# Two x tiles by DMA transposes, one tile's statistics on ScalarE, and finer-grained products at the head of a token-mixing MLP kernel

## The chip, the cores and the metric

The kernel runs on one core of a Trainium2 chip. The metric is the device time of one execution in microseconds, as the median of several runs. The engines are named as in the profile: PE (TensorE, matmuls), PEld (its weight loads), DVE (VectorE), ACT (ScalarE), POOL (GpSimd) and SP (SyncE, which here only issues DMAs).

## The reference

```python
B, S, D, F = 1, 2048, 512, 1792          # everything in bf16

def reference(x, w1, w2, w3, w4):
    h = _gelu(_layernorm(x, axis=-1) @ w1)             # D -> D
    c = D // 4                                         # four groups of 128 channels,
    g0 = h[..., 0*c:1*c] shifted by +1 along S         # zero padded at the ends
    g1 = h[..., 1*c:2*c] shifted by -1
    g2 = h[..., 2*c:3*c] shifted by +2
    g3 = h[..., 3*c:   ] shifted by -2
    x1 = x + jnp.concatenate([g0, g1, g2, g3], axis=-1) @ w2
    return x1 + _gelu(_layernorm(x1, axis=-1) @ w3) @ w4
```

(The four shifts are written here in words; the original pads and slices.)

## The kernel before

The 2048 rows are 16 tiles of 128 rows. Row p*16+t belongs to partition p of tile t, so that a shift along S by one or two rows is, but for the edges, a step to the neighbouring tile. The work of a tile goes through these stages:

- **Statistics** on DVE: `stats` (L325, "st") gives partial means and variances, `aggr` (L328, "ag") merges them. **Power** on POOL: `rstd_pool` ("rs") adds epsilon (L349) and raises to -0.5 (L358). **Normalization** on DVE: `norm` (L378) writes the bf16 tile `xn`; for the second layer norm some tiles are normalized by ACT (L373) instead, for which POOL also makes a negative mean (L354) and its product with the power (L363).
- **Transposes** of `xn` into `xT`, by one of two paths. `peT` (L400, "tp") transposes four 128x128 blocks on PE into a PSUM bank, and `evacT` on ACT (L412, "evA") copies the bank to SBUF. `dmaT` (L388, "dT") issues one DMA transpose from SP's queue. Before, tiles 0 to 7 go over PE and tiles 8 to 15 by DMA.
- **First products** `mm1` (L451): for a pair p of tiles (2p and 2p+1), 16 matmuls of 256 columns each into two PSUM banks, in four groups by output chunk. Pair 0 has a form of its own, `mm1_by_input` (L467), which goes through the input chunks in the outer loop, so that it can begin with the first half of w1. `gelu1` on ACT (L495, L501, L512) writes the result to `hT`.
- **Second products** `mm2` (L526): for a tile, four matmuls of 512 columns that read the four channel groups of `hT` at the neighbouring tiles' places (`window`), summed in one PSUM bank. `add1` on DVE (L538) adds x and writes `x1`.
- **Second layer norm**: the same statistics on `x1`, in the order of tiles 2, 3, ..., 15, 0, 1 (numbered 16 to 31 in the program), all transposed by DMA into `x1T`.
- **Wide products**: `mm3` (L553) with w3 for 512 rows at a time (s = 0 to 3), `gelu2` (L566) on ACT, and `mm4` (L579) with w4; `add2` (L593) adds `x1` and SP writes the tile out. Before it can begin, `mm3` needs all of w3 and the first four tiles of `x1T`.

There is no scheduler: each engine does its operations in the order in which the Python program records them. For the head (up to the first layer norm's last tile) this order is written by hand as one string, `HEAD`, a list of steps such as `st 4` or `m1 2 0 1` (pair 2, banks from 0, output chunk 1), which all engines share; each engine takes from it what is its own, in order. What follows it is a sequence of Python calls. `emit` finds what each operation depends on, from the tiles that it reads and writes, and puts a semaphore wait ahead of it (L134) where the dependence isn't known to be met. A PSUM bank or a buffer that is used again waits for the readers of its last use.

All loads stand in SP's queue, in this order: x tiles 0 to 3 one by one, tiles 4 and 5, w1 in two halves, tiles 6 and 7, tiles 8 to 11, tiles 12 to 15, w2; then the DMA transposes of `xT`, w3, the DMA transposes of `x1T`, and w4 in four parts between the last of these. `keep_warm` (L611) fills the start of PE with matmuls on constants: 12 at the beginning and 3 more once the variance of tile 3 is there.

Of the kernel before, what the change touches and what calls it, by code (L numbers as in the profile page):

```python
# [5 lines left out]
P = 128  # L6
ACT_F = mybir.ActivationFunctionType
ALU = mybir.AluOpType
# [152 lines left out]
st 0; ag 0; rs 0 1; st 1; ag 1; rs 1 1; st 2; st 3; ag 2; ag 3; warm 3 3 1; rs 2; norm 1; norm 0;  # L161
tp 1 5; tp 0 4; st 4; evA 1; norm 2; norm 3; evA 0; tp 2 6; tp 3 7; st 5; ag 4; ag 5; m1i 0 0 0;
evA 3; rs 4; m1i 0 0 1; evA 2; m1i 0 0 2; st 6; m1i 0 0 3; norm 4; m1 1 4 3; norm 5; g1 0;
tp 4 6; st 7; m1 1 4 0; ag 6; ag 7; tp 5 7; rs 6; evA 4; m1 1 4 1; st 9; evA 5; m1 1 4 2; st 8;
norm 7; m1 2 0 1; ag 8; ag 9; g1 1; m1 2 0 3; rs 8; norm 6; tp 7 7; st 11; m1 2 0 2; evA 7;
tp 6 6; norm 8; m1 2 0 0; ag 11; evA 6; m2 2 4 0; m2 2 4 1; st 10; m1 3 2 2; norm 9; ag 10; g1 2;
m1 3 2 0; rs 10; st 13; m1 3 2 1; m1 3 2 3; st 12; m2 2 4 2; dT 8; m2 2 4 3; norm 11; ag 13;
norm 10; g1 3; m2 3 5 0 1 2 3; st 14; ag 12; dT 9; rs 12; st 15; m2 4 6 0 1 2 3; ag 14; ag 15;
m1 4 0 3; rs 14; dT 11; m1 4 0 1; norm 13; m1 4 0 0; add 3; norm 14; dT 10; m2 5 7 0 1 2 3;
add 2; m1 4 0 2; norm 12; norm 15; dT 13; g1 4; dT 12; dT 14; dT 15  # L170
# [3 lines left out]
def bass_standalone__mixer_s_mlp__prompt_kernel(  # L174
# [26 lines left out]
    with ExitStack() as es:  # L201
# [11 lines left out]
        ident = sb("ident", [P, P], BF16)  # L213
        xn = sb("xn", [P, NXN, D], BF16)
# [61 lines left out]
        def consts():  # L276
# [8 lines left out]
            pr.op("pool", "eps", lambda e: e.memset(eps_c[:], LN_EPS), w=[g_eps])  # L285
            pr.op("pool", "nh", lambda e: e.memset(neghalf[:], -0.5), w=[g_nh])
# [44 lines left out]
        g_sd = {}  # L331
# [34 lines left out]

        def norm(eng, q):
# [3 lines left out]
            if eng == "act":  # L371
# [3 lines left out]
                      r=[g, g_nmr[q], g_rstd[q]], w=[g_xn[q]])  # L375
            else:
# [82 lines left out]
        def mm1_by_input(p, b, dcs):  # L459

            if p not in g_y:
                g_y[p] = ([bank[b + i].new() for i in range(DC)], b)
            for dc in dcs:
                def f(e, dc=dc):
                    for fc in range(DC):
                        dst = ps[:, 512 * (b + fc) : 512 * (b + fc) + 256]
                        ins = e.matmul(dst, w1_sb[:, dc, P * fc : P * (fc + 1)],  # L467
# [50 lines left out]
        def mm2(t, b, js=(0, 1, 2, 3)):  # L518

            if t not in g_o:  # L520
                g_o[t] = (bank[b].new(), b)
# [253 lines left out]
```

## Time and profile before

| what | value |
|---|---|
| median of 3 runs | 138.96 us (138.89 to 139.28) |
| the profiled execution's own time | 139.09 us |
| its span in the profile | 137.3 us |
| PE busy | 131.9 us (96%), 689 recorded instructions |
| DVE busy | 51.6 us (38%) |
| ACT busy | 50.0 us (36%) |
| POOL busy | 18.3 us (13%) |
| DMA | 12.16 MB, 20119 packets |
| granted TensorE clock | 9 in all 40 slices |

The span is the time between the first and the last instruction that the profiler saw; the execution's own time is 1.8 us longer, for what lies around it. Times in views are microseconds from the start of the span. A line of a timeline gives the start, the duration, the engine, the source line, the operation, the tiles written and read, the shapes and how many instructions are merged; in square brackets stands the idle time before and what ended it. Matmuls are pipelined: a matmul's recorded duration is longer than the distance to the next one, so distances of starts, not durations, give what one costs PE. A few matmul records are missing in the trace, so that counts such as x31 for 32 occur.

### The profile page before, as it was taken

The page shows a single profiled execution, that of the slowest core. Times are in us where ns is not written, and L with a number is a line of the kernel's source. Part 1 is how long each engine was busy: PE and PEld are TensorE (multiplying, and loading weights), DVE is VectorE, ACT ScalarE, POOL GpSimd, SP SyncE. Part 2 cuts the span into 40 slices and gives each one's busy share as a digit, 9 for nine tenths or more (in the row PEclk, how much of TensorE's full clock was granted, in tenths as well). Part 3 has the DMA queues.
Part 4 walks back from the last instruction along what each step waited for, and adds up shares of the span by engine and source line. Part 5 has one row for each costly group of instructions (what it writes and reads, how often), then busy time and mean ns, then how long its engine had stood idle before and what let it go on. Part 6 is the DMA issues. An engine that isn't in the chain of part 4 may idle for free.

```text
span 137.3 us, 1790 instructions
## 1 busy us (share of the span) xinstructions
PE 131.9 (96%) x689; PEld 66.5 (48%) x701; DVE 51.6 (38%) x125; ACT 50.0 (36%) x60; POOL 18.3 (13%) x52
## 2 busy tenths in 40 slices
PE   7879999999999999999999999999999999999993
PEld 3267847664444444444444444444444444444452
DVE  0989899999976620000232000023200002232222
ACT  4068622399545555552000555300055530000000
POOL 2542442464312200000000000000000000000000
PEclk9999999999999999999999999999999999999999
DMA  4996144589955599300111100011110001111121
GB/s 106 289 283 238 27 93 82 111 261 351 133 100 113 83 287 257 103 5 0 38 38 38 38 0 5 0 38 38 38 38 0 5 0 38 38 38 38 38 74 41
DMA packets 20119, 12.16 MB, mean 89 GB/s; under 512 B 13712, under 2 KB 19088, under 8 KB 20112
## 3 DMA queue, kind: packets, MB, share of 16 engines
q1 hardware_dynamic: 19968, 12.03, 33.6%
q8 instruction: 5, 0.08, 0.3%
q10 hardware_dynamic: 144, 0.03, 0.1%
q14 instruction: 2, 0.02, 0.0%
HBM read 6.82 MB, written 2.10 MB: 65 GB/s over the span
## 4 chain that ended last, share of the span: by engine, by line
PE 83%; DVE 8%; DMA 4%; POOL 1%; issue 1%; DVEq 0%
PE ps L579 35%; PE ps L553 35%; PE ps L526 8%; PE ps L451 5%; DVE st L325 5%; DVE xn L378 2%; DMA x_sb<-in_x_dram 2%; DMA xT<-xn 2%; POOL rstd L358 1%; DVE mv L328 1%; POOL vpe L349 0%; DVE o_sb L593 0%; DVEq L134 0%
## 5 line engine op out<-in xcount | busy, mean ns | idle before, releaser
L579 PE MATMUL ps<-w_sb,h2T 128*128 128x512 bf16 (+2 forms) x234 | 48.7, 366 | 0.2
L553 PE MATMUL ps<-x1T,w_sb 128*128 128x512 bf16 x219 | 48.6, 379 | 0.3
L566 ACT ACTIVATE h2T<-ps 128x1024 bf16<-128x1024 f32 x28 | 28.6, 1023 | 44.8 <-PE ps L553 44.8
L593 DVE TENSOR_TENSOR o_sb<-ps,x_sb 128x512 bf16<-128x512 f32 (+2 forms) x17 | 11.2, 660 | 75.0 <-PE ps L579 75.0
L579 PEld LDWEIGHTS ps<-w_sb,h2T 128*128 128x128 bf16 x238 | 22.8, 98 | 25.9
L553 PEld LDWEIGHTS ps<-x1T,w_sb 128*128 128x128 bf16 x224 | 21.9, 98 | 26.4
L325 DVE BATCH_NORM_STATS2 st<-x_sb 128x6 f32<-128x512 bf16 x32 | 20.7, 675 | 2.3 <-DMA x_sb<-in_x_dram 2.3
L526 PE MATMUL ps<-w_sb,hT 128*128 128x512 bf16 x61 | 14.3, 379 | 0.2
L451 PE MATMUL ps<-xT,w_sb 128*128 128x256 bf16 x112 | 14.0, 273 | 0.3 <-DMA xT<-xn 0.3
L451 PEld LDWEIGHTS ps<-xT,w_sb 128*128 128x128 bf16 x112 | 10.6, 98 | 3.1 <-issue 0.7
L358 POOL TENSOR_TENSOR rstd<-vpe,neghalf 128x2 f32<-128x2 f32 (+1 forms) x17 | 11.8, 695 | 1.0
L538 DVE TENSOR_TENSOR x_sb<-ps,x_sb 128x512 bf16<-128x512 f32 x16 | 10.3, 678 | 0.3 <-PE ps L526 0.2
L378 DVE TENSOR_SCALAR xn<-x_sb,mv,rstd 128x512 bf16<-128x512 bf16 x22 | 8.3, 405 | 5.2 <-POOL rstd L358 5.0
L526 PEld LDWEIGHTS ps<-w_sb,hT 128*128 128x128 bf16 x64 | 6.2, 98 | 6.3 <-ACT hT L512 0.3
L373 ACT ACTIVATE xn<-x_sb,nmr,rstd 128x512 bf16<-128x512 bf16 x10 | 7.6, 807 | 3.3 <-POOL nmr L363 3.3
L512 ACT ACTIVATE hT<-ps 128x1024 bf16<-128x1024 f32 x6 | 6.1, 1019 | 6.1 <-PE ps L451 6.0
L349 POOL TENSOR_SCALAR vpe<-mv 128x2 f32<-128x2 f32 (+1 forms) x17 | 3.9, 229 | 27.3 <-DVE mv L328 27.2
L412 ACT ACTIVATE xT<-ps 128x512 bf16<-128x512 bf16 x8 | 4.5, 603 | 5.9 <-PE ps L400 5.9
L611 PE MATMUL ps<-const-bfloat16-1.0 128*128 128x512 bf16 x15 | 5.4, 522 | 0.9 <-PEq L760 0.8
L328 DVE BATCH_NORM_AGGREGATE mv<-st 128x2 f32<-128x6 f32 x32 | 4.9, 172 | 0.1
L400 PE MATMUL ps<-ident,xn 128*128 128x128 bf16 x32 | 3.0, 221 | 1.2 <-DVE xn L378 1.2
L611 PEld LDWEIGHTS ps<-const-bfloat16-1.0 128*128 128x128 bf16 x15 | 1.8, 127 | 4.0 <-issue 3.2
(18 smaller groups left out, 12.8 us busy)
## 6 DMA issues: line engine op xcount, KB each, us to landing
w_sb<-in_w_dram SPq DMA_DIRECT2D x4, 512.0 KB, 4.8
out_dram<-o_sb SPq DMA_DIRECT2D x15, 128.0 KB, 1.8
w_sb<-in_w_dram SPq DMA_DIRECT2D x1, 1792.0 KB, 7.3
x_sb<-in_x_dram SPq DMA_DIRECT2D x2, 512.0 KB, 7.5
w_sb<-in_w_dram SPq DMA_DIRECT2D x3, 256.0 KB, 4.1
x_sb<-in_x_dram SPq DMA_DIRECT2D x4, 128.0 KB, 2.5
x_sb<-in_x_dram SPq DMA_DIRECT2D x2, 256.0 KB, 4.1
x1T<-xn SPq DMA_TRANSPOSE x16, 3.6
```

The lines of the kernel that those rows point to most:

```text
L325: pr.op("dve", f"st{q}", lambda e: e.bn_stats(st6[:, q, :], a), r=[g], w=[g_st[q]])
L358: lambda e: e.tensor_tensor(rstd[:, q : q + n], vpe[:, q : q + n], neghalf[:, 0:n], ALU.pow),
L373: lambda e: e.activation(xn[:, s, :], a, ACT_F.Identity, bias=nmr[:, q : q + 1], scale=rstd[:, q : q + 1]),
L378: lambda e: e.tensor_scalar(xn[:, s, :], a, mv[:, q, 0:1], rstd[:, q : q + 1], ALU.subtract, ALU.mult),
L451: ins = e.matmul(dst, w1_sb[:, dc, P * fc : P * (fc + 1)], xT[:, dc, 256 * p : 256 * (p + 1)], start=(dc == 0), stop=(dc == DC - 1))
L526: ins = e.matmul(bankap(b), hT[:, j, c : c + P], w2_sb[:, j, :], start=(j == 0), stop=(j == DC - 1))
L538: lambda e: e.tensor_tensor(x1_sb[:, t, :], bankap(b), x_sb[:, t, :], ALU.add),
L553: ins = e.matmul(bankap(b + i), w3_sb[:, dc, P * fc : P * (fc + 1)], x1T[:, dc, 512 * s : 512 * (s + 1)], start=(dc == 0), stop=(dc == DC ...
L566: pr.op("act", f"g2_{s}_{fp}", lambda e: e.activation(o, a, ACT_F.Gelu_apprx_tanh), r=gens, w=[g])
L579: ins = e.matmul(ps[:, 512 * b : 512 * b + n], h2T[:, fc, s % 2, P * i : P * (i + 1)], w4_sb[:, fc, c0 : c0 + n], start=(fc == 0), stop=(f ...
L593: lambda e: e.tensor_tensor(o_sb[:, s, 0:n], ps[:, 512 * b : 512 * b + n], x1_sb[:, t, c0 : c0 + n], ALU.add),
L611: ins = e.matmul(bankap(b), ones[:, 0:P], ones, start=True, stop=True)
```

## The change

- Tiles 6 and 7 are transposed by DMA (`dT 7` and `dT 6`, in this order, ahead of `dT 8`) instead of by PE and ACT. Their `tp` and `evA` steps are gone.
- Tile 2's statistics are made by ACT: `sum_act` ("sum") passes the tile with an accumulating output, POOL makes the negative mean, `dev_act` ("dev") passes it again as squares of the deviation, accumulating. POOL makes variance plus epsilon of it (`vpe_dev`, "vpd"), the same for tile 3 from DVE's statistics (`vpe_bn`, "vp"), and raises both to -0.5 in one instruction (`pow2`, "pw"). Tile 2's normalization on DVE then adds the negative mean in place of subtracting the mean.
- The first products of tiles 0 and 1 are made one tile at a time: `mm1_tile_by_input` ("m1x"), 16 matmuls of 128 columns per tile, in place of `mm1_by_input`.
- Second products in the head may be recorded as single groups: `mm2` counts its groups, so that the first and last of a tile's four set the start and stop marks, whatever group they are. The head has the second products of tiles 2 to 7 in such pieces.
- The order in `HEAD` is new throughout. The warm-up has 11 matmuls at the beginning instead of 12, and the 3 further ones stand behind tile 0's transposes on PE.
- Two small constants (`eps`, `nh`) are set by DVE instead of POOL. w4 is loaded in two parts of 7 chunks instead of four (4, 4, 4 and 2).

```diff
 HEAD = """
-st 0; ag 0; rs 0 1; st 1; ag 1; rs 1 1; st 2; st 3; ag 2; ag 3; warm 3 3 1; rs 2; norm 1; norm 0;
-tp 1 5; tp 0 4; st 4; evA 1; norm 2; norm 3; evA 0; tp 2 6; tp 3 7; st 5; ag 4; ag 5; m1i 0 0 0;
-evA 3; rs 4; m1i 0 0 1; evA 2; m1i 0 0 2; st 6; m1i 0 0 3; norm 4; m1 1 4 3; norm 5; g1 0;
-tp 4 6; st 7; m1 1 4 0; ag 6; ag 7; tp 5 7; rs 6; evA 4; m1 1 4 1; st 9; evA 5; m1 1 4 2; st 8;
-norm 7; m1 2 0 1; ag 8; ag 9; g1 1; m1 2 0 3; rs 8; norm 6; tp 7 7; st 11; m1 2 0 2; evA 7;
-tp 6 6; norm 8; m1 2 0 0; ag 11; evA 6; m2 2 4 0; m2 2 4 1; st 10; m1 3 2 2; norm 9; ag 10; g1 2;
-m1 3 2 0; rs 10; st 13; m1 3 2 1; m1 3 2 3; st 12; m2 2 4 2; dT 8; m2 2 4 3; norm 11; ag 13;
-norm 10; g1 3; m2 3 5 0 1 2 3; st 14; ag 12; dT 9; rs 12; st 15; m2 4 6 0 1 2 3; ag 14; ag 15;
-m1 4 0 3; rs 14; dT 11; m1 4 0 1; norm 13; m1 4 0 0; add 3; norm 14; dT 10; m2 5 7 0 1 2 3;
-add 2; m1 4 0 2; norm 12; norm 15; dT 13; g1 4; dT 12; dT 14; dT 15
+st 0; ag 0; rs 0 1; st 1; ag 1; sum 2; norm 0; rs 1 1; tp 0 4; st 3; dev 2; ag 3; vpd 2; evA 0;
+norm 1; vp 3; warm 3 3 1; tp 1 5; st 4; m1x 0 0 0; pw 2 2; m1x 0 0 1; evA 1; st 5; m1x 0 0 2;
+norm 3; m1x 0 0 3; norm 2; ag 4; tp 3 7; ag 5; m1x 1 0 0; rs 4; m1x 1 0 1; st 7; tp 2 6;
+m1x 1 0 2; m1x 1 0 3; st 6; evA 2; ag 7; ag 6; rs 6; norm 4; evA 3; norm 5; tp 4 6; g1 0;
+m1 1 4 1; tp 5 7; norm 7; m1 1 4 2; evA 5; st 8; m1 1 4 3; evA 4; m1 1 4 0; st 9; ag 8; ag 9;
+m1 2 0 3; rs 8; norm 6; m1 2 0 1; g1 1; st 10; m1 2 0 2; norm 8; m1 2 0 0; dT 7; m2 2 4 0;
+m2 2 4 1; st 11; ag 10; m2 2 4 2; ag 11; m2 3 5 0; g1 2; rs 10; norm 9; m2 3 5 2; m2 4 6 2;
+m2 5 7 2; dT 6; st 13; m2 3 5 1; m2 2 4 3; m2 5 7 0; st 12; m2 3 5 3; m2 4 6 0; norm 11; ag 12;
+dT 8; m1 3 2 2; add 3; ag 13; m1 3 2 3; rs 12; m1 3 2 0; add 2; dT 9; norm 10; m1 3 2 1;
+m2 6 4 2; m2 6 4 0; st 14; m2 7 5 2; m2 4 6 1; g1 3; st 15; dT 11; m1 4 0 0; norm 13; m2 6 4 1;
+ag 15; ag 14; m2 4 6 3; rs 14; norm 12; m1 4 0 2; m2 5 7 1; dT 10; m1 4 0 3; norm 14; m1 4 0 1;
+m2 5 7 3; norm 15; m2 7 5 0; dT 13; g1 4; dT 12; dT 14; dT 15
 """
...
-            pr.op("pool", "eps", lambda e: e.memset(eps_c[:], LN_EPS), w=[g_eps])
-            pr.op("pool", "nh", lambda e: e.memset(neghalf[:], -0.5), w=[g_nh])
+            pr.op("dve", "eps", lambda e: e.memset(eps_c[:], LN_EPS), w=[g_eps])
+            pr.op("dve", "nh", lambda e: e.memset(neghalf[:], -0.5), w=[g_nh])
...
+        def sum_act(q):
+            ...
+            pr.op("act", f"sq_sum{q}",
+                  lambda e: e.activation(sink[:], a, ACT_F.Identity, accum_out=tot[:, q, 0:1]),
+                  r=[g], w=[gs, g_sum[q]])
+            pr.op("pool", f"nm{q}",
+                  lambda e: e.tensor_scalar(nmean[:, q : q + 1], tot[:, q, 0:1], -1.0 / D, None,
+                                            ALU.mult),
+                  r=[g_sum[q]], w=[g_nm[q]])
+        def dev_act(q):
+            ...
+            pr.op("act", f"sq_dev{q}",
+                  lambda e: e.activation(sink[:], a, ACT_F.Square, bias=nmean[:, q : q + 1],
+                                         scale=1.0, accum_out=tot[:, q, 1:2]),
+                  r=[g, g_nm[q]], w=[gs, gd])
+        def vpe_dev(q):
+            ...
+                  lambda e: e.tensor_scalar(vpe[:, q : q + 1], tot[:, q, 1:2], 1.0 / D, LN_EPS,
+                                            ALU.mult, ALU.add),
+        def vpe_bn(q):
+            ...
+                  lambda e: e.tensor_scalar(vpe[:, q : q + 1], mv[:, q : q + 1, 1], LN_EPS, None,
+                                            ALU.add),
+        def pow2(q, n):
+            ...
+                  lambda e: e.tensor_tensor(rstd[:, q : q + n], vpe[:, q : q + n],
+                                            neghalf[:, 0:n], ALU.pow),
...
+            elif q in g_nm:
+                pr.op(eng, f"norm{q}",
+                      lambda e: e.tensor_scalar(xn[:, s, :], a, nmean[:, q : q + 1],
+                                                rstd[:, q : q + 1], ALU.add, ALU.mult),
...
+        def mm1_tile_by_input(t, b, dc):
+            p = t // 2
             if p not in g_y:
                 g_y[p] = ([bank[b + i].new() for i in range(DC)], b)
+            def f(e):
+                for fc in range(DC):
+                    o = 512 * (b + fc) + P * (t % 2)
+                    ins = e.matmul(ps[:, o : o + P], w1_sb[:, dc, P * fc : P * (fc + 1)],
+                                   xT[:, dc, P * t : P * (t + 1)],
+                                   start=(dc == 0), stop=(dc == DC - 1))
+                return ins
...
         def mm2(t, b, js=(0, 1, 2, 3)):
             if t not in g_o:
                 g_o[t] = (bank[b].new(), b)
+                n_o[t] = 0
+            n0 = n_o[t]
+            n_o[t] += len(js)
...
-                                   start=(j == 0), stop=(j == DC - 1))
+                                   start=(n == 0), stop=(n == DC - 1))
...
-        keep_warm(12, 3)
+        keep_warm(11, 3)
...
         ln2a(0), ln2b(0)
-        mm2s(4, 4)
+        mm2(6, 4, (3,))
+        mm2(7, 5, (1, 3,))
...
-            load_w4(2 * (k - 10), 4)
+            if k < 14:
+                load_w4(7 * (k - 10) // 2, 7)
         wide(0, [2, 3])
-        load_w4(12, FC - 12)
```

## The prediction

> **What bounds the kernel now.** I read the page's chain first, for the engine that sets the end; then the timeline of PE, for the place where it still waits; then the timelines of DVE and of SP's queue, for what it waits for there.
>
> ```profile
> span 137.3 us, 1790 instructions
> ...
> PE 83%; DVE 8%; DMA 4%; POOL 1%; issue 1%; DVEq 0%
> ```
>
> The chain is PE's for 83%. DVE's 8% and the DMA's 4% lie in the first 20 us. The timeline of PE there:
>
> ```profile
> 6.76 0.72 PE L400 MATMUL ps<-ident,xn 128*128 128x128 bf16 x8 [0.48 <-DVE xn L378]
> 8.18 0.72 PE L400 MATMUL ps<-ident,xn 128*128 128x128 bf16 x8 [0.70 <-DVE xn L378]
> ...
> 10.95 0.40 PE L400 MATMUL ps<-ident,xn 128*128 128x128 bf16 x4
> 11.18 0.60 PE L451 MATMUL ps<-xT,w_sb 128*128 128x256 bf16 x4
> ...
> 19.82 1.47 PE L451 MATMUL ps<-xT,w_sb 128*128 128x256 bf16 x12 [0.25 <-DMA xT<-xn]
> ...
> 27.65 1.89 PE L526 MATMUL ps<-w_sb,hT 128*128 128x512 bf16 x8
> 29.38 1.91 PE L451 MATMUL ps<-xT,w_sb 128*128 128x256 bf16 x16
> 31.12 7.07 PE L526 MATMUL ps<-w_sb,hT 128*128 128x512 bf16 x31
> ```
>
> Starts give prices: a 128-column transpose is (11.18-10.95)/4 = 0.056 us, a 256-column product (31.12-29.38)/16 = 0.109, a 512-column one (29.38-27.65)/8 = 0.216. PE waits for DVE at 6.3 and 7.5, for ScalarE's copy at 12.87 (below), for a transpose at 19.4 to 19.82, and not again before the wide products (L553) begin at 38.03; behind those it is full to the end. So the change, which touches the first 38 us, is worth what it moves that 38.03.
>
> ```profile
> 12.86 0.77 PEld L451 LDWEIGHTS ps<-xT,w_sb 128*128 128x128 bf16 x8 [0.26 <-ACT xT L412]
> ...
> 3.30:13.00 9.70, 8.37 (x68) 5.29 (x67) 8.90 (x24) 4.38 (x10) 4.35 (x10) 1.00 0.90 287
> ```
>
> In the table by stretches (PE, PEld, DVE, ACT, POOL), DVE works 8.90 of the 9.70 us from 3.3 to 13.0: the statistics and normalizations are the early bound, ScalarE is half idle. SP's queue is a second chain, nearly as late:
>
> ```profile
> 15.52 11.04 SPq L388 DMA_TRANSPOSE xT<-xn  x8
> 26.60 0.58 SPq L262 DMA_DIRECT2D w_sb<-in_w_dram  x1
> 28.12 17.16 SPq L388 DMA_TRANSPOSE x1T<-xn  x12
> ```
>
> Eight transposes hold SP 1.27 us each (one 1.64), then w3 is issued at 26.60, and the first four of x1T lie behind it. By the trace's landings w3 is in at 33.94 and the fourth at 37.48, 0.3 us before PE loads its weights at 37.81.
>
> **Check of the sum on the kernel before.** From 12.87 PE has six pairs of first products, 96 x 0.109 = 10.5; tiles 6 and 7's transposes, 8 x 0.056 = 0.45; 64 second products, 64 x 0.216 = 13.8; the wait at 19.4, 0.4. 12.87 + 25.15 = 38.02, against 38.03.
>
> **The change, part by part.** (1) Tile 2's statistics leave DVE (one of 0.60 by starts, and a 0.1 merge), and the order there is new. I walk it with before's distances: statistics to the next 0.60 (its own merge 0.73), merge 0.10 to 0.11, normalization 0.32, and 0.11 from POOL's power to a normalization that waits for it (10.37 to 10.48). st0 3.31, ag0 4.04, st1 4.14, ag1 4.83 as now. norm0 waits for the power that ended at 5.20: 5.31. st3 5.63, ag3 6.36, norm1 6.46, st4 6.78, st5 7.38, norm3 7.98, norm2 8.30, ag4 8.62, ag5 8.73, st7 8.83 (its tile landed at 8.55), st6 9.43, ag7 10.03, ag6 10.14, norm4 10.24, done 10.65. Tile 4's transposes start 0.06 later, as tile 1's do now: 10.7.
>
> (2) norm3 also needs a power made of tile 2's deviation on ScalarE and tile 3's variance. ScalarE's sum starts when tile 2 lands, 4.2. With s for one accumulating pass: the POOL mean 0.22, second pass s, two POOL steps of 0.31, the power 0.71, and handovers of 0.04 to 0.11 put norm3 at 6.1 + 2s or later. No row has an accumulating pass. Lower end: the 128x512 copy (L412), 0.60. Upper end: the pass with two pointers (L373), 0.81, plus a whole small ACTIVATE (L601), 0.20, for the accumulator: 1.01. A gain from it is excluded, since a whole tile must pass. I take 0.9, nearer to L373, because the second pass has a pointer: norm3 at 7.9, hidden by DVE's own 7.98. At 1.01 everything behind is 0.15 later; at 1.3 the gain is gone. Queued behind the two passes is tile 0's copy, which ends about 7.0 where tile 1's transposes keep PE until 7.1.
> The Trainium skill (ScalarE: Activation LUTs, What ACT_TABLE_LOAD costs) gives 186 ns + 0.833 per column and 93 ns per pointer: 0.80 for L373, which the row's 0.807 confirms, so 0.61 and 0.71 here with the accumulator's reading unpriced. By it my 0.9 is on the dear side, and the sum would be the same.
>
> (3) Products of tiles 0 and 1 by tile: 32 of 128 columns in place of 16 of 256. Same columns: 32 x 0.056 = 1.8 against 1.75, if products follow each other as transposes do. Upper end 32 x 0.109 = 3.5. They lie between 7.1 and 9.7, and PE then waits for norm4 until 10.7; that wait covers 0.9 us of extra cost. Were they 0.109, I find tile 4 at 11.1 and half a microsecond lost. I take 0.056, the row of the same width. The warm-up (11 matmuls, then 3 between the transposes of tiles 0 and 1) lies in waits; the two memsets moved to DVE lie in its wait for x, 2.3 us.
>
> (4) Tiles 6 and 7 by DMA: PE loses 0.45 us, ScalarE two copies of 0.60. SP gains two transposes, 2.6 us, ahead of all later ones and of w3. norm7 waits for its power, runs at 11.5 and lets the first out at 12.0 (before: 15.52); behind it on SP are nine more and w3. norm6 follows at 13.3, its transpose lands some 2.6 later, 16.4; PE needs the pair at about 17.2 (10.7, 0.45, two pairs 3.5, twelve second products 2.6). Cover 0.8. Going down the queue at 1.31 each, with two waits for DVE of 0.4 and 0.2, w3 goes out at 26.2, 0.4 earlier than now; with before's 10.9 from w3 to the fourth of x1T, 37.1.
>
> (5) Second products in single groups: the same 64 x 0.216; they fill PE until tile 6's transpose is in. Tiles 6 and 7 reuse the banks of 2 and 3, so they wait for add2 and add3, which DVE now does earlier; I find that even to 0.05 us. w2 must be in at 14.65 instead of 15.3; it lands at 14.24. w4 in two loads instead of four is issued from 45 us on, for products at 62: nothing.
>
> **Sum.** After tile 4's start PE has 8 x 0.056 + 112 x 0.109 + 64 x 0.216 = 26.45, and I add 0.2 for joints that each wait a twentieth: 10.7 + 26.65 = 37.35. I keep 0.13 back for the more broken order: 37.48, which is 0.55 earlier than 38.03, and later than SP's 37.1. The profiled execution has 139.09 around its span of 137.3, so the sum gives 138.54 there; the median is 0.13 below that execution, hence 138.4.
>
> **The rivals.** *Accumulating passes dear.* At s from 1.1 to 1.3 norm3 slips 0.3 to 0.7 and so does all behind it. For: no row shows them. Against: the rows that bound them. 138.7 to 138.95, no change. 0.17.
> *w2 late.* The trace shows PE's instruction fetch, one packet of 16 KB, at 15.32 for 1.4 us; PE reaches the same instruction count about 14.0 in the new order. If the DMA engine that fetches still holds part of w2, w2 lands 0.8 to 1.0 late and PE stands 0.4 to 0.6. Against: eleven of w2's sixteen parts are in by 13.0. 138.8 to 139.0, no change. 0.10.
> *SP's queue becomes the bound (slower).* Ten transposes at 1.31 just fit. It decides from w3 at 27.0 on: plus 10.9 that passes 37.9. If the new ones cost 1.64, or each waits a little for its normalization, w3 goes out at 27.6, the fourth of x1T lands at 38.5, PE starts 0.55 after 38.03: 139.5. For: margins of 0.3 and one issue of 2.2 us in the trace. Against: seven of eight take 1.27. 0.12.
> *The clock falls.* PE is idle for more of 4.9 to 10.7 (about 45%, now a third). The first matmuls start 0.427 apart until 4.1, twice the later 0.216; 3.4 us at half speed behind 10.7 would cost 1.7: 140.1. Against: PEclk stays at 9 through waits of 0.48 and 0.70. 0.06.
> The Trainium skill (TensorE: Matmul & The Clock Gate, Part 1: The HAM clock gate) has the gate close only after an idle window of about 3.4 us; the longest wait I find is 0.9, and by that rule this rival falls away.
> A second table load for the squares (1.28 each) would be in the changed program's order; it has one load.
>
> **Numbers.** About 0.3% (0.42 us) is what a measurement of this kernel can tell from no change. Forecast 0.55, alone 138.2 to 138.55; faster 0.55, same 0.17 + 0.10 = 0.27, slower 0.12 + 0.06 = 0.18. The range goes from 138.1 (the 0.2 for joints and the 0.13 both at nothing) to 139.4, most of the way into the SP case; the clock and the worst of SP stay out.
>
> **What would show it.** norm4 before 10.4 and tile 4's transposes at 10.7, at the end of PE's last large wait; both accumulating passes under 0.95; 128-column products 0.056 apart; SP's first transpose at 12.0 and w3 at 26.2; wide products at 37.3 to 37.6 without a wait for x1T. Wrong if PE waits for w2 near 14.7, for tile 6's transpose near 17.2, or for x1T near 37.5, or if norm3 waits for POOL beyond 8.4.

## The result, and the profile after

The change makes the kernel slower: 139.37 us (138.71 to 140.21, 17 runs) against 138.89 (138.38 to 139.28, 17 runs) of the kernel before, ratio 1.0043 with an interval of 1.0025 to 1.006. The profiled execution took 139.72 us around a span of 137.9. One run each of two kernels below ("statistics of 6, 7 free" and "free, mean by ScalarE") had a granted clock of 0.988 and took nearly 2 us longer, and no number given for them includes it.

The end of the chain line of the page, with the span:

```profile
span 137.9 us, 1808 instructions
...
PE 79%; DVE 7%; DMA 7%; POOL 2%; SPq 2%; issue 1%; DVEq 0%
```

PE has lost 4% of the chain, and most of that has gone to the DMA (7% for 4%). The timeline of PE shows where:

```profile
8.31 1.32 PE L525 MATMUL ps<-xT,w_sb 128*128 128x128 bf16 x16 [0.67 <-DMA w_sb<-in_w_dram]
9.47 0.39 PE L457 MATMUL ps<-ident,xn 128*128 128x128 bf16 x4
9.69 0.61 PE L525 MATMUL ps<-xT,w_sb 128*128 128x128 bf16 x8
10.14 0.39 PE L457 MATMUL ps<-ident,xn 128*128 128x128 bf16 x4
...
11.50 0.40 PE L457 MATMUL ps<-ident,xn 128*128 128x128 bf16 x4 [0.53 <-DVE xn L435]
...
25.40 0.81 PE L586 MATMUL ps<-w_sb,hT 128*128 128x512 bf16 x3
26.50 1.92 PE L508 MATMUL ps<-xT,w_sb 128*128 128x256 bf16 x16 [0.29 <-DMA xT<-xn]
...
38.64 0.59 PE L613 MATMUL ps<-x1T,w_sb 128*128 128x512 bf16 x2
```

Tile 4's transposes start at 11.50 (forecast 10.7; before 10.95), pair 6's products wait at 26.50 for a DMA transpose, and the wide products start at 38.64 (forecast 37.48; before 38.03). From there to the end both kernels take 99.25 us, so the whole difference lies in the first 38. By starts the wait at 26.50 is 0.45: three 512-column products from 25.40 end their share at 26.05. The timeline of DVE and the chain of waits, read forwards, name the cause of both:

```profile
7.10 1.28 DVE L329 BATCH_NORM_STATS2 st<-x_sb 128x6 f32<-128x512 bf16 x2
...
8.93 0.24 DVE L332 BATCH_NORM_AGGREGATE mv<-st 128x2 f32<-128x6 f32 x2
9.63 1.29 DVE L329 BATCH_NORM_STATS2 st<-x_sb 128x6 f32<-128x512 bf16 x2 [0.46 <-DMA x_sb<-in_x_dram]
10.84 0.30 DVE L332 BATCH_NORM_AGGREGATE mv<-st 128x2 f32<-128x6 f32 x2
11.06 0.71 DVE L435 TENSOR_SCALAR xn<-x_sb,mv,rstd 128x512 bf16<-128x512 bf16 x2
```

```profile
4.05 5.56 DMA x_sb<-in_x_dram
9.61 0.02 issue
9.63 1.29 DVE st L329 x2
...
23.01 3.44 DMA xT<-xn
26.45 0.04 issue
26.50 1.92 PE ps L508 x16
```

The load of tiles 6 and 7 goes out at 4.05 and lands at 9.61; in the first profile of before it landed at 8.54. DVE, done with its merges, waits for it, then makes both statistics and both merges, and only then tile 4's normalization (11.06, before 10.48). The same work carries on to the transposes on SP's queue, and that of tile 12, issued at 23.01, lands 3.44 us later, when PE has been ready for 0.45.

SP's queue, the second chain of the prediction:

```profile
12.88 14.22 SPq L445 DMA_TRANSPOSE xT<-xn  x10
27.14 0.58 SPq L266 DMA_DIRECT2D w_sb<-in_w_dram  x1
```

The first transpose goes out at 12.88 (forecast 12.0), w3 at 27.14 (forecast 26.2, before 26.60). The fourth of x1T lands at 38.16, half a microsecond ahead of the wide products, which do not wait for it.

### The profile page after: what moved, and what is told of

Read it like the earlier page. It is cut to its first block, busy times and chain, and to the rows that moved or that the text cites. A ratio compares the mean times of both kernels' runs of the same rounds, so it can differ in the third digit from the quotient of the medians.

```text
span 137.9 us, 1808 instructions
## 1 busy us (share of the span) xinstructions
PE 132.2 (96%) x696; PEld 66.6 (48%) x708; DVE 50.9 (37%) x125; ACT 50.3 (36%) x62; POOL 19.0 (14%) x52
## 4 chain that ended last, share of the span: by engine, by line
PE 79%; DVE 7%; DMA 7%; POOL 2%; SPq 2%; issue 1%; DVEq 0%
PE ps L639 35%; PE ps L613 35%; PE ps L586 6%; DMA x_sb<-in_x_dram 4%; DVE st L329 4%; PE ps L508 3%; DMA xT<-xn 2%; DVE xn L435 2%; POOL rstd L364 2%; SPq L259 2%; DVE x_sb L598 1%; DVE mv L332 1%; SPq L266 1%; POOL vpe L355 1%; DVE o_sb L653 0%
## 5 line engine op out<-in xcount | busy, mean ns | idle before, releaser
L329 DVE BATCH_NORM_STATS2 st<-x_sb 128x6 f32<-128x512 bf16 x31 | 20.0, 680 | 2.8 <-DMA x_sb<-in_x_dram 2.8
L508 PEld LDWEIGHTS ps<-xT,w_sb 128*128 128x128 bf16 x112 | 10.7, 98 | 3.3 <-DMA xT<-xn 0.8
L364 POOL TENSOR_TENSOR rstd<-vpe,neghalf 128x2 f32<-128x2 f32 (+1 forms) x16 | 11.1, 694 | 0.9
L469 ACT ACTIVATE xT<-ps 128x512 bf16<-128x512 bf16 x6 | 3.3, 592 | 2.9 <-PE ps L457 2.9
L457 PE MATMUL ps<-ident,xn 128*128 128x128 bf16 x24 | 2.5, 233 | 0.9 <-DVE xn L435 0.9
```

Of the source, the lines that this page charges most:

```text
L329: pr.op("dve", f"st{q}", lambda e: e.bn_stats(st6[:, q, :], a), r=[g], w=[g_st[q]])
L364: lambda e: e.tensor_tensor(rstd[:, q : q + n], vpe[:, q : q + n], neghalf[:, 0:n], ALU.pow),
L508: ins = e.matmul(dst, w1_sb[:, dc, P * fc : P * (fc + 1)], xT[:, dc, 256 * p : 256 * (p + 1)], start=(dc == 0), stop=(dc == DC - 1))
```

## The experiments

Three theories were put up. **A:** the loads do not land at a fixed time; the new order of DVE puts the statistics of tiles 6 and 7 ahead of tile 4's normalization and so depends on their load. In its wider form, PE's new order also depends on w1's second half. **B:** TensorE waits near 26 us for tile 12's DMA transpose, because SP's queue has two transposes more. **C:** POOL's mean of tile 2 (0.40 us, queued behind a power) delays the normalization of tile 3. "Before" was run beside the kernels on each chip, and five groups of runs on four chips follow. "Free" in a name means that a step reads a tile that is already there, so that it has nothing to wait for, and the right values of its own tiles are left out. The last column is the median span less that of before on the same chip, in us; it is given because the time outside the span is not the same for all kernels (last section). The unedited changed kernel was run in the first group alone, where its ratio was 1.0075 in place of the result's 1.0043; on the other chips a kernel can be set beside it by ratios only, and these are uncertain by about this difference.

| kernel | median us | ratio to before (95%) | span |
|---|---|---|---|
| changed, again | 139.94 | 1.0075 (1.0048 to 1.0103) | +1.2 |
| statistics of 6, 7 free | 139.07 | 1.0020 (0.9995 to 1.0044) | +0.3 |
| 6, 7 on PE again | 140.04 | 1.0079 (1.0047 to 1.0110) | +1.3 |
| tile 2 on DVE again | 140.41 | 1.0087 (1.0058 to 1.0117) | +1.0 |
| before, statistics of 6, 7 free | 138.59 | 0.9989 (0.9972 to 1.0006) | -0.15 |
| one statistic ahead | 139.55 | 1.0074 (1.0048 to 1.0100) | +0.6 |
| transposes ahead of w1 | 139.76 | 1.0070 (1.0045 to 1.0096) | +1.0 |
| both of these | 139.71 | 1.0088 (1.0057 to 1.0118) | +0.75 |
| no transpose of tile 6 | 139.22 | 1.0020 (1.0000 to 1.0040) | +0.15 |
| free, and no transpose of 6 | 139.21 | 1.0020 (1.0002 to 1.0038) | +0.1 |
| before, again | 138.87 | 0.9994 (0.9978 to 1.0010) | -0.2 |
| tile 6 on PE, 7 by DMA | 139.71 | 1.0062 (1.0038 to 1.0086) | +0.55 |
| pair 6 free | 139.24 | 1.0025 (1.0005 to 1.0045) | +0.3 |
| free, mean by ScalarE | 139.32 | 1.0037 (1.0013 to 1.0062) | +0.1 |
| all three free | 139.47 | 1.0061 (1.0034 to 1.0088) | +0.25 |
| one statistic ahead, mean by ScalarE | 139.05 | 1.0024 (1.0001 to 1.0047) | 0.0 |
| all four free | 138.63 | 1.0011 (0.9992 to 1.0030) | -0.15 |
| all real edits | 138.92 | 1.0033 (1.0014 to 1.0051) | +0.3 |

### First group: what of the change costs the time

The changed kernel unchanged, for a second profile.

> The changed kernel as it is, for a second trace. Theory A (late loads: in the new order the statistics of tiles 7 and 6 stand on DVE ahead of tile 4's normalization, so the landing of that load, 9.61 us in the profiled execution and 8.55 in the one of before, is on the path): the time follows the landing, tile 4's transposes start at 10.9 where the load is in by 8.9 and one for one later beyond it; ratio to before about 1.003 to 1.006 again. Theory B (SP's queue with two more transposes): whatever the landing, PE waits again for a transposed pair near 26 us. Theory C (POOL's mean of tile 2 took 0.40 and stood behind a power): tile 3's normalization at 8.2 to 8.3 again.

Measured 139.94. The load of tiles 6 and 7 landed at 9.10, DVE's statistics began at 9.12, PE waited again near 26 (0.40), and the wide products began at 38.07. The profile is of the fastest of the 12 executions (139.17), so that it shows less than the usual loss.

The same with nothing to wait for at tiles 6 and 7:

```diff
-            a, g = src(q)
+            a, g = src(q - 6 if q in (6, 7) else q)
```

> Changed kernel, but the statistics of tiles 6 and 7 are made of tiles 0 and 1 (so tiles 6 and 7 are normalized with the wrong mean and variance), which takes the wait for their load away and leaves every instruction. A: tile 4's normalization at 10.5 whatever the load does; about 0.1 us faster than the changed kernel in an execution with a late w1 (whose wait takes over), up to 0.5 with a late tile 6 alone, 0 with early loads; ratio to before 0.999 to 1.002. B: no change beyond what the earlier start of the transposes gives (0.3 at most); PE waits near 26 again. C: no change, 1.004.

Measured 139.07, 0.87 us below the kernel above on the same chip; the two intervals do not meet. Its profile has the latest landing of all, 10.25, and DVE does not notice:

```profile
8.78 1.26 DVE L329 BATCH_NORM_STATS2 st<-x_sb 128x6 f32<-128x512 bf16 x2
9.95 0.30 DVE L332 BATCH_NORM_AGGREGATE mv<-st 128x2 f32<-128x6 f32 x2
10.17 0.70 DVE L435 TENSOR_SCALAR xn<-x_sb,mv,rstd 128x512 bf16<-128x512 bf16 x2
```

This is as A says. Tile 4's transposes nevertheless start at 11.24, and the wide products at 38.13, no earlier than in the profile above, so that the two profiles do not show the gain of the medians. In PE's timeline another load is late:

```profile
8.95 0.62 PE L525 MATMUL ps<-xT,w_sb 128*128 128x128 bf16 x8 [0.86 <-DMA w_sb<-in_w_dram]
...
11.24 0.38 PE L457 MATMUL ps<-ident,xn 128*128 128x128 bf16 x4 [0.33 <-ACT xT L469]
```

The products that need w1's second half (landed at 8.90) stand ahead of tile 2's transposes; tile 4's take over that bank when ScalarE has copied it. Hence the wider form of A.

Tiles 6 and 7 on TensorE and ScalarE again, in the new order:

```diff
-... m1 2 0 0; dT 7; m2 2 4 0;
+... m1 2 0 0; tp 7 7; tp 6 6; evA 7; evA 6; m2 2 4 0;
-m2 5 7 2; dT 6; st 13; ...
+m2 5 7 2; st 13; ...
```

> Changed kernel with tiles 6 and 7 transposed on PE and copied by ScalarE again, 8 transposes of 128 in SP's queue. A: no gain, PE has 0.45 us more work and about 0.3 to 0.5 more waits for ScalarE: 0.6 to 0.9 slower than the changed kernel, ratio 1.008 to 1.010. B: SP's queue starts at about 15.6 with 8 transposes, the wait near 26 us (0.45) is gone and w3 goes out no later: 0 to 0.4 slower, ratio 1.004 to 1.007. C: as A.

Measured 140.04, as slow as the changed kernel. The wait near 26 is gone, and 0.40 for ScalarE at 18.55 stands in its place: in time, moving the two tiles' transposes to the DMA is about even. (Tiles 6 and 7 landed at 10.12 in that profile, so that the load held it up as well.)

Tile 2's statistics on DVE again:

```diff
-st 0; ag 0; rs 0 1; st 1; ag 1; sum 2; norm 0; rs 1 1; tp 0 4; st 3; dev 2; ag 3; vpd 2; evA 0;
-norm 1; vp 3; warm 3 3 1; tp 1 5; st 4; m1x 0 0 0; pw 2 2; ...
+st 0; ag 0; rs 0 1; st 1; ag 1; norm 0; rs 1 1; tp 0 4; st 2; st 3; ag 2; ag 3; evA 0;
+norm 1; rs 2; warm 3 3 1; tp 1 5; st 4; m1x 0 0 0; ...
```

> Changed kernel with tile 2's statistics on DVE again (ScalarE's two passes and their POOL steps gone). A: where the load of tiles 6 and 7 is late DVE only waits less for it, no change; with early loads 0.35 slower; ratio 1.004 to 1.007. B: no change or 0.3 slower. C: DVE has 0.7 more and POOL is free earlier: tile 3's normalization at 8.6 to 8.7 instead of 8.3, so 0.3 slower unless the load hides it; if ScalarE's passes cost more than they save, it is faster, 1.002.

Measured 140.41, 0.47 above the changed kernel, but with overlapping intervals, and with a span 0.2 below it. Normalization of tile 4 again came 1.44 behind the landing (9.28, 10.72): with the load in the way, what ScalarE takes from DVE is worth nothing that shows.

### Second group: a control, and two changes of order

The control: the same edit of the statistics in the kernel before.

> The kernel before, with the statistics of tiles 6 and 7 made of tiles 0 and 1 (left out: the right statistics of these two tiles), so that nothing on VectorE's early path waits for the load of tiles 6 and 7. Control of the same edit in the changed kernel, which made that one 0.86 us faster. Theory A (in the old order only one of the two statistics stands ahead of the normalization of tile 4, and a landing up to about 9.8 us costs nothing): within 0.3 us of before, ratio 0.997 to 1.001. Rival (the load hurts both orders alike, and the loss of the change lies elsewhere): 0.6 to 0.9 us faster than before, ratio about 0.994.

138.59 against 138.69, no difference. The wait whose removal gained 0.87 in the new order costs the old one nothing measurable.

Then tile 6's statistics behind the normalizations of tiles 4 and 5:

```diff
-... m1x 1 0 3; st 6; evA 2; ag 7; ag 6; rs 6; norm 4; evA 3; norm 5; tp 4 6; g1 0;
-m1 1 4 1; ...
+... m1x 1 0 3; evA 2; ag 7; rs 7 1; norm 4; evA 3; norm 5; tp 4 6; g1 0;
+st 6; ag 6; rs 6 1; m1 1 4 1; ...
```

> The changed kernel with tile 6's statistics moved from ahead of the normalization of tile 4 to behind that of tile 5, and the powers of tiles 7 and 6 made one by one. Nothing is left out. Theory A (two statistics and two merges that wait for the late load stand ahead of the normalization of tile 4): tile 4's transposes start 0.3 to 0.7 us earlier than in the changed kernel in a profile with the same landing, and the time is 0.2 to 0.5 us below the changed kernel on the same chip. Theory B (what is lost is the wait for a DMA transpose near 26 us): no gain, and 0.1 to 0.3 us slower where tile 6's transpose, which now goes out later, is waited for. Theory C (the POOL chain): no change.

139.55, a span 0.6 over before's. The trace did what A says, the normalization of tile 4 0.85 us behind the landing (9.75, 10.60) in place of 1.45; in time it is 0.2 below the next kernel, whose edit gained nothing, and 0.4 in the span, with overlapping intervals. The changed kernel itself was not run on this chip.

```diff
-... st 5; m1x 0 0 2;
-norm 3; m1x 0 0 3; norm 2; ag 4; tp 3 7; ag 5; m1x 1 0 0; rs 4; m1x 1 0 1; st 7; tp 2 6;
-m1x 1 0 2; m1x 1 0 3; st 6; evA 2; ... norm 4; evA 3; norm 5; ...
+... st 5;
+norm 3; norm 2; ag 4; tp 3 7; tp 2 6; m1x 0 0 2; m1x 0 0 3; ag 5; m1x 1 0 0; rs 4; m1x 1 0 1; st 7;
+m1x 1 0 2; m1x 1 0 3; st 6; evA 3; ... norm 4; evA 2; norm 5; ...
```

> The changed kernel with the transposes of tiles 3 and 2 ahead of those products of tile 0 that need the second half of w1. Nothing is left out. Theory A as told so far (only the load of tiles 6 and 7 counts): no change against the changed kernel, within 0.2 us. Its wider form (the second half of w1 landed at 7.8 to 9.4 us, and where it is late, everything on TensorE and the copies behind it is late as well): 0.1 to 0.4 us faster. Theories B and C: no change.

139.76. No gain: w1's second half (8.84) no longer decided, but the load of tiles 6 and 7 did (9.53, normalization of tile 4 at 10.97). PE stood in a new place, 0.73 us at 18.79, for a late transpose: tile 6's, issued at 14.50 and landed at 18.75.

Both edits together, whose diff is the sum of the two:

> The changed kernel with both edits: tile 6's statistics behind the normalization of tile 5, and the transposes of tiles 3 and 2 ahead of the products that need the second half of w1. Nothing is left out. Theory A in its wider form: 0.4 to 0.8 us faster than the changed kernel, so at or a little below the time of the kernel before (138.3 to 138.9). Theory B: no gain, since the wait for the DMA transpose near 26 us stays. Theory C: no change.

139.71, a miss of the forecast: normalization of tile 4 stood 0.85 behind a landing of 9.89, so there was nothing left to gain in that profile, and the wait near 26 stayed (0.36).

### Third group: the transposes

```diff
-m2 5 7 2; dT 6; st 13; ...
+m2 5 7 2; st 13; ...
...
+            s = 2 if p == 3 else p
...
-                                       xT[:, dc, 256 * p : 256 * (p + 1)],
+                                       xT[:, dc, 256 * s : 256 * (s + 1)],
```

> The changed kernel without the DMA transpose of tile 6: the first products of tiles 6 and 7 read the transposed tiles 4 and 5 (left out: their own). SP's queue has one transpose less ahead of those of tiles 8 to 15. Theory B (SP's queue sets when the transpose of tile 12 lands, and TensorE waits for it near 26 us): that transpose goes out 1.3 to 1.7 us earlier, the wait of 0.4 to 0.45 near 26 us is gone, from tile 4's transposes to the wide products it is 26.65 to 26.9 us in place of 27.1, and the time is 0.2 to 0.45 us below the changed kernel's (ratio to before about 1.002 to 1.005). Theory A (the late load of tiles 6 and 7) alone: no change, ratio about 1.007.

139.22, a ratio as B foretold it, but the trace denies B's reason:

```profile
26.36 1.92 PE L509 MATMUL ps<-xT,w_sb 128*128 128x256 bf16 x16 [0.26 <-DMA xT<-xn]
```

The wait is still there, 0.43 by starts. Tile 8's transpose left at 15.85 (after: 16.45), since it now waited for DVE's normalization (15.41), tile 12's at 22.87 (after: 23.01), and it again took 3.44 to land. By this trace the number of transposes alone does not make it late: DVE's pace, SP's 1.3 us each and the late landing all have a part. Why the ratio is lower is not shown.

Both suspects away (this edit and that of the statistics):

> Both suspects taken away in the changed kernel: statistics of tiles 6 and 7 made of tiles 0 and 1, and no DMA transpose of tile 6 (its products and tile 7's read the transposed tiles 4 and 5). Left out: the right values of these two tiles. If A and B together are the whole loss: 0.5 us or more below the kernel with the free statistics alone, that is 138.2 to 138.7 us, ratio 0.996 to 1.000. Theory A alone: the same as with the free statistics alone, 139.1 us, ratio about 1.002. If something else is lost as well, the ratio stays over 1.000 in spite of both.

139.21, no better than either alone. Against the kernel just above (139.22 on the same chip) the free statistics gain nothing in time, which speaks against A as the whole cause. The trace has no wait at 26 and tile 4's transposes at 10.92, again 2.34 behind w1's second half (8.58), and the wide products at 37.72, where the kernel just above has 38.49; but it is of the fastest of its 12 executions (138.77), and the other of a slower one than its median (139.56).

The kernel before, for a second profile:

> The kernel before, unchanged, for a second profile of it. Theory A: the load of tiles 6 and 7 lands later than the 8.54 us of the first profile (the other kernels' profiles lie at 9.1 to 10.25), tile 0 earlier than the 3.29 us, and the time is all the same 138.7 us within 0.15, because the old order depends on the first and hardly on the second. If the load lands near 8.5 again, the old order itself makes it early, and theory A is wrong on chance. Theory B says nothing of it.

138.87, 0.02 over the expected range. In DVE's timeline the two profiles of before, the first and this one, answer for A:

```profile
9.18 0.66 DVE L325 BATCH_NORM_STATS2 st<-x_sb 128x6 f32<-128x512 bf16 x1
10.48 0.73 DVE L378 TENSOR_SCALAR xn<-x_sb,mv,rstd 128x512 bf16<-128x512 bf16 x2 [0.64 <-POOL rstd L358]
```

```profile
9.87 0.69 DVE L325 BATCH_NORM_STATS2 st<-x_sb 128x6 f32<-128x512 bf16 x1 [0.86 <-DMA x_sb<-in_x_dram]
10.48 0.72 DVE L378 TENSOR_SCALAR xn<-x_sb,mv,rstd 128x512 bf16<-128x512 bf16 x2
```

The load landed at 9.85 here, 1.3 later than in the profile that the forecast was made from, w1's second half at 9.13 (7.60 there). Tile 4's normalization is at 10.48 in both. In the first profile it waited for POOL's power, with tile 0 landed 0.39 later than here; here the one statistic ahead of it waited for the load. Against the 10.10 of the kernel with free statistics, where tile 0 landed as here (2.91), the old order has lost 0.38 to the load, and not the 1.3.

```diff
-... m1 2 0 0; dT 7; m2 2 4 0;
+... m1 2 0 0; dT 7; tp 6 6; evA 6; m2 2 4 0;
-m2 5 7 2; dT 6; st 13; ...
+m2 5 7 2; st 13; ...
```

> The changed kernel with tile 6 transposed by TensorE and copied by ScalarE again, tile 7 by DMA as changed. Nothing is left out. Theory B: SP's queue is one transpose shorter, the wait near 26 us is gone (0.4), four transposes come back on TensorE (0.22) and one copy of 0.6 on ScalarE, where it may delay a GELU by up to 0.4: between 0.2 us faster and 0.2 us slower than the changed kernel. Theory A alone: 0.2 to 0.5 us slower than the changed kernel.

139.71. No wait near 26, and nothing gained: four transposes came back, and a wait of 0.26 at 16.95.

### Fourth and fifth group: does the forecast sum come out

Pair 6 made free of the wait, with all transposes in place:

```diff
+            s = 5 if p == 6 else p
...
-                                       xT[:, dc, 256 * p : 256 * (p + 1)],
+                                       xT[:, dc, 256 * s : 256 * (s + 1)],
```

> The changed kernel in which the first products of tiles 12 and 13 read the transposed tiles 10 and 11 (left out: their own), so that TensorE does not wait for tile 12's transpose near 26 us; all DMA transposes are still made. Theory B (that wait costs its whole length): the wait is gone, from tile 4's transposes to the wide products it is 26.65 to 26.8 us in place of 27.1, and the time is 0.3 to 0.45 us below the changed kernel's, ratio to before 1.002 to 1.004. Theory A alone: no change, ratio 1.004 to 1.007.

139.24, in the range of B. The wait moved: PE stood 0.57 at 18.18 for tile 6's transpose (issued 14.04, landed 18.14), and tile 4's transposes to the wide products took 27.19, no less than with the wait at 26. So the range was met, but not for B's reason.

```diff
-            pr.op("pool", f"nm{q}",
-                  lambda e: e.tensor_scalar(nmean[:, q : q + 1], tot[:, q, 0:1], -1.0 / D, None,
-                                            ALU.mult),
+            pr.op("act", f"nm{q}",
+                  lambda e: e.activation(nmean[:, q : q + 1], tot[:, q, 0:1], ACT_F.Identity,
+                                         scale=-1.0 / D),
```

This with the free statistics:

> The changed kernel with the statistics of tiles 6 and 7 made of tiles 0 and 1 (left out: the right ones) and with tile 2's mean made by ScalarE between its two passes in place of POOL. Theory C (POOL's mean, 0.40 us and queued behind a power, costs time of its own): the normalization of tile 3 starts 4.7 us behind the first statistics in place of 4.95, that of tile 4 6.95 behind in place of 7.2, and the time is 0.1 to 0.3 us below that of the kernel with the free statistics alone, ratio 1.000 or a little below. Theories A and B without C: no change, ratio 1.002.

139.32. Set beside the free statistics alone, on another chip, the ratio is no better (1.0037 for 1.0020), though the span is 0.2 nearer to before's; outside the span this kernel has 0.2 more. So it is not shown whether C costs time. Tile 3's normalization moved from 5.0 to 4.56 us behind the first statistics, as C says, and tile 4's from 7.2 to 6.74, but tile 4's transposes (10.61) are again 2.34 behind w1's second half (8.27), and tile 9's transpose, landed at 20.51, costs PE 0.58.

This, the free statistics and the free pair 6 together:

> All three taken away in the changed kernel: statistics of tiles 6 and 7 of tiles 0 and 1, tile 2's mean by ScalarE, products of tiles 12 and 13 from the transposed tiles 10 and 11 (left out: the right values of these four tiles). If A, B and C are the whole of the loss, the forecast sum comes out: wide products 34.2 to 34.5 us behind the first statistics, 138.2 to 138.45 us, ratio 0.995 to 0.998. If something else is lost, a later start of the wide products than that shows where.

139.47, a miss in time. In the profile the wide products start 34.55 us behind the first statistics, just beyond what was expected, although w1's second half, landed at 8.83, holds tile 4's transposes until 11.17, again 2.34 later. The rest of the miss lies ahead of that and outside: tile 0 landed at 3.40, and the time outside the span is 2.1 us in place of 1.83. In span, too, it gains next to nothing over the free pair 6 alone (0.25 over before's for 0.3, same chip), so that here again the free statistics do not show in the medians.

A version with nothing left out: one statistic ahead, and the mean by ScalarE.

> A version that leaves nothing out: the changed kernel with tile 6's statistics behind the normalization of tile 5, and tile 2's mean made by ScalarE. Theory A: normalization of tile 4 at the landing of tiles 6 and 7 plus 0.85 us or at 6.95 us behind the first statistics, whichever is later; with landings of 9.1 to 10.2 that is 0.1 to 0.4 us earlier than in the changed kernel. The wait near 26 us stays (theory B). Together 139.0 to 139.5 us, ratio 1.001 to 1.005: not faster than before.

139.05, as expected: its span equals before's, and its time does not beat it. Tile 4's normalization came 0.85 us behind the landing (9.09, 9.94), but its transposes again 2.34 behind w1's second half (8.29, 10.63).

The transposes ahead of w1 as well, and pairs 3 to 6 free (`s = 2 if 3 <= p <= 6 else p`), on top of all three:

> The changed kernel with four things taken away: the statistics of tiles 6 and 7 are made of tiles 0 and 1; tile 2's mean is made by ScalarE; the transposes of tiles 3 and 2 stand ahead of the products that need the second half of w1; the first products of tiles 6 to 13 all read the transposed tiles 4 and 5, so that TensorE waits for no DMA transpose (left out: the right values of tiles 6 to 13). If the late loads, POOL's mean and the DMA transposes are the whole loss (theories A in its wider form, B, C): tile 4's transposes 7.2 to 7.4 us behind the first statistics, from there to the wide products 26.65 to 26.8 us, so these 33.9 to 34.2 behind the first statistics (before: 34.5 to 34.9 in three profiles), 138.0 to 138.4 us, ratio 0.994 to 0.998. If the ratio is 1.000 or more with that place of the wide products, the time is lost outside what the early stage shows.

138.63 against 138.56, ratio 1.0011 with 1 in the interval, a span 0.15 below before's: the loss is gone, the forecast gain of 0.55 does not come. Its profile, 0.68 above its own median, has the wide products 35.05 us behind the first statistics, later than expected, and shows the next load in the row:

```profile
7.21 1.29 DVE L329 BATCH_NORM_STATS2 st<-x_sb 128x6 f32<-128x512 bf16 x2 [0.85 <-DMA x_sb<-in_x_dram]
```

Tile 4's statistics wait for tile 4's load (7.18; 5.99 to 6.87 elsewhere).

And all edits that leave nothing out (one statistic ahead, the mean by ScalarE, the transposes ahead of w1):

> A version that leaves nothing out: the changed kernel with tile 6's statistics behind the normalization of tile 5, tile 2's mean made by ScalarE, and the transposes of tiles 3 and 2 ahead of the products that need the second half of w1. Tile 4's transposes at the landing of tiles 6 and 7 plus 1.29 us or 7.4 us behind the first statistics, whichever is later; the waits for DMA transposes stay (0.25 to 0.45). 138.7 to 139.1 us, ratio 0.999 to 1.003: at best the time of the kernel before.

138.92 against 138.56, as expected. No version of the new order beats the kernel before.

## Why the prediction was wrong

The landings, from the traces, against what followed:

| profile | tile 0 | w1, 2nd half | tiles 6, 7 | tile 4 normalized | its transposes | wide products |
|---|---|---|---|---|---|---|
| before, first | 3.29 | 7.60 | 8.54 | 10.48 | 10.95 | 38.03 |
| before, again | 2.90 | 9.13 | 9.85 | 10.48 | 10.94 | 37.81 |
| before, free statistics | 2.91 | 8.55 | 9.25 | 10.10 | 10.57 | 37.46 |
| changed, first | 3.37 | 8.96 | 9.61 | 11.06 | 11.50 | 38.64 |
| changed, again | 2.90 | 7.77 | 9.10 | 10.54 | 10.98 | 38.07 |
| changed, free statistics | 2.96 | 8.90 | 10.25 | 10.17 | 11.24 | 38.13 |

**The step that failed is (1), its term "st7 8.83 (its tile landed at 8.55)".** It took a landing from one execution as a property of the kernel, with 0.28 us to spare. What the runs showed in its place: over 20 profiles tiles 6 and 7 landed at 8.54 to 10.25 us, w1's second half at 7.60 to 9.43, and the profile of before that the forecast rests on had the earliest of both, and a late first tile besides (3.29; 15 of the 20 lie at 2.88 to 3.02), which made the old order look slow and the new one free. In eight profiles with the new order tile 4's normalization comes 1.44 to 1.45 us behind that landing, with one statistic ahead (four profiles) 0.85: the load sets it. From there it goes on to the wide products, which start 29.03 and 28.97 us behind that landing in the two profiles of the changed kernel, and 28.8 to 29.5 in the other six. In the two of before it is 29.49 and 27.96: there the landing was 1.3 later and the wide products were not. In the old order POOL's power is later than the one statistic until the load lands at about 9.5 (an estimate: 10.10 less the 0.63 from landing to normalization in the second profile of before), so it loses little.

That is the mechanism, and the traces show it. The experiment for it is the free statistics: 0.87 us in the first group, and nothing in the old kernel. Its share of the loss is less certain. The changed kernel had a ratio of 1.0075 there and 1.0043 in the result, against which the same 1.0020 is worth some 0.3 us (an estimate from these ratios); and added to the kernel without tile 6's transpose, or, together with the mean by ScalarE, to the one with pair 6 free, the free statistics gained nothing in the medians. The load is issued at 4.05 in every profile. It landed at 8.54, 9.25 and 9.85 in three profiles of the old order and at 8.96 to 10.25 in 17 of the new one; whether the new order also delays it is not shown by these.

**In the profiled execution the account closes.** Wide products came at 38.64 in place of 37.48, 1.16 late. Tile 4's transposes: 0.80, of which 0.09 is tile 0's landing, 0.23 POOL's mean (0.40 for the 0.22 taken, and queued behind a power), and 0.48 the load, which ends later than both, so that without POOL's share the sum would be the same. Behind them: 0.45 for tile 12's transpose, 0.04 in the products, less the 0.13 kept back.

**Step (4)** looked at tile 6's pair, w3 and x1T, and not at pair 6, where the queue binds. The rival "SP's queue becomes the bound" had the sign and nearly the time (139.5), but not the place: w3 at 27.14 and the fourth of x1T at 38.16 were awaited by nobody; tile 12's transpose was. That its time fits is luck. The first transpose was 0.9 late, as everything behind the load, tile 6's issue took 1.87 for 1.31, and tile 12's landing 3.44 for the 2.5 of most.

**Right were** the passes of ScalarE, the pitch of the 128-column products (8 in 0.45 from 9.69 to 10.14, 0.056 each), w2 (landed at 13.97, no wait), the granted clock (9 in all 40 slices again), the single table load, and PE's sum: from 11.50 to 38.64 less the wait it is 26.69, forecast 26.65. The passes, in ScalarE's timeline of the changed kernel:

```profile
4.17 0.63 ACT L379 ACTIVATE sink<-x_sb 128x512 bf16<-128x512 bf16 x1 [1.95 <-DMA x_sb<-in_x_dram]
4.70 0.19 ACT L379 ACTIVATION_READ_ACCUMULATOR sink<-x_sb 128x1 f32 x1
5.81 0.72 ACT L391 ACTIVATE sink<-x_sb,nmean 128x512 bf16<-128x512 bf16 x1 [0.92 <-POOL nmean L382]
```

With the reading of the accumulator they are 0.72 and 0.81 long, under the 0.9 taken. The estimates worked out from the Trainium skill (ScalarE: Activation LUTs, What ACT_TABLE_LOAD costs) were 0.61 and 0.71 for the passes, and the trace's 0.63 and 0.72 agree.

**What stays open.** The wider form of A rests on one distance in five traces (tile 4's transposes 2.34 us behind w1's second half) and on the fifth group, where much else is changed too; the transposes-ahead edit alone gained nothing. It is not shown why the free statistics gained 0.87 us in one group and nothing in two others, why the ratio is lower without tile 6's transpose although the wait stayed, nor why the changed kernel lost 0.43% in the result and 0.75% in the first group. With all four suspects away, some 0.4 of the forecast gain is still missing in the span; a wait for tile 4's load, seen in one profile, may be part of it.

## What to carry to other kernels

A landing in one profile is a sample, not a constant: before an order is tightened around a load, ask for the slack that it has now and how much of it the new order spends, and take a second profile of the kernel before. A step that waits for a load belongs behind the steps that do not, even where in the one trace it fits. Where a queue gets more to do, check each consumer behind it, not only the first and the last.

## What the runs showed of the hardware

The load of tiles 6 and 7, issued at 4.05 us behind the same loads in all 20 profiles, lands up to 1.7 us apart (8.54 to 10.25), while what follows the early stage is steady: 99.2 to 99.3 us from the wide products to the end in every profile.

Transposes mostly land 2.5 us after their issue. In 16 of the 17 profiles of the new order, one that was in flight when a fetch of instructions began took about 4 us or more (3.97 to 4.36); in the other one it took 3.06. In the changed kernel it is tile 7's, issued at 12.88, which took 4.15, with a fetch of 16 KB on the DMA queue q8 at 14.84 (1.13 us); tile 12's took 3.44 there, with a fetch of 8 KB on q14 at 24.27 (0.68 us). In two other kernels tile 6's took 4.25 and tile 9's 4.23, with q8's fetch at 16.47 and 17.98. In the first profile of before q8's fetch began at 15.32, ahead of the first transpose (15.52), which took 2.76; one of the other seven took 3.48, with q14's fetch at 23.02. The profile names the queue of a fetch and not the engine; q8's, which the prediction calls PE's, is put down to PE because PE has by far the most instructions. That the fetch is the cause is read from the times alone and was not tried. The Trainium skill (Runtime: NRT & Kernel Launch, Instruction fetch mechanics) calls the cost of such a refill mostly hidden, and that passage does not speak of other transfers in flight; here it is these that land late.

The time outside the span goes with the kernel: in the median 1.82 to 1.85 us for before, the changed kernel and eight others, 1.95 to 2.2 for eight (2.08 with all four free), and up to 3.4 in single runs. The eight are the ones whose edit touches POOL's own instructions (the mean by ScalarE, tile 6's statistics moved with powers made one by one, tile 2's statistics on DVE again); but before's POOL instructions differ from the changed kernel's too, and its time outside does not. What the time is made of is not shown, and it is as large as some of the differences sought.
